# One pool of eight PSUM banks, with dependencies by bank, in a one-core kernel of windowed attention and channel mix

## The chip, the core and the metric

The kernel runs on one core of a Trainium2 chip. The metric is the device time in microseconds of one execution; the lower the better. TensorE (PE) multiplies matrices, ScalarE (ACT) applies functions, VectorE (DVE) does elementwise work, GpSimd (POOL) and SyncE (SP) mainly issue DMAs here. PE writes its results to PSUM, which has eight banks of 512 float32 in each of 128 partitions; ACT and DVE read them from there.

## The reference

Eight batches of eight heads, 576 positions, 64 values a head. Attention looks back over a window of 128 positions and adds a bias that falls with distance; its output is the input of a channel mix with a squared ReLU and a sigmoid gate.

```python
scores = scale * np.matmul(q, k.transpose(0, 1, 3, 2))
scores = np.where((rel >= 0) & (rel < 128), scores + bias, -1e9)
attn = softmax(scores)                       # over the last axis
x = (attn @ v)                               # to [8, 576, 512]
x_prev = x shifted by one position
xk = mu_k * x + (1 - mu_k) * x_prev
xr = mu_r * x + (1 - mu_r) * x_prev
k = np.maximum(xk @ w_k, 0)                  # 512 -> 1024
v = (k * k) @ w_v                            # 1024 -> 512
out = v / (1 + exp(-(xr @ w_r)))
```

## The kernel before

The work of a batch is cut into four pairs of heads. For a pair, PE makes q and k transposed (`qk_quad`, L1070), the scores in two halves of up to 512 columns for each of two heads (`scores`, L698; matmuls at L726, which have 64 rows and run two at a time, and for batch 0 a bias matmul at L713), ACT takes their exponential (L740), DVE multiplies by a table of the bias and the window (L753), PE multiplies by v (`attend`, L759, matmul L781, here called AV), DVE divides by the row sums (L787, L793), PE transposes the result (L820, L837) and ACT copies it (L696). DVE makes the shifted mixes xk and xr (L880, L887). The channel mix (L968) goes over 13 stretches of 256 to 512 positions: eight groups of k matmuls (L983), each with a Relu on ACT (L990) and a square on ACT (L962) or DVE (L964); then for each 128 positions the r matmuls (L1001) with a Tanh on ACT (L1008), the v matmuls (L1017), and one DVE instruction (L1022) that joins the two before the store. At the start PE runs 90 filler matmuls (`warm`, L687) in places of the order.

The order of PE, ACT and DVE is written out by hand: the lists `ORDER` (L22 to L71) name operations by number, and the planner (L88) gives each engine the next one of its list as soon as its operands and buffers are there, so that its clock and its buffers decide which buffer an operation gets (`pick`, L130, `take`, `give`), not the order. The order of DMA issues on POOL and SP is its own choice. An operation asks for buffers by `Hold(class)`. PSUM has two classes: `p2`, the two tiles `duo0` and `duo1` of two banks each, for scores and AV, and `p1`, the four tiles `uno0` to `uno3` of one bank, for the rest (L369 to L383). The framework makes an instruction wait for earlier instructions on other engines that use the same tile. `SS` (L298) says for which batches the two halves of a pair's scores are separate operations in the lists: for none. So both halves stand in one operation, which needs both `duo` tiles.

The lines that the prediction speaks of are those named above and ACT's first table load, which the profile puts at L696.

Of the kernel before, what the change touches and what calls it, by code (L numbers as in the profile page):

```python
# [9 lines left out]
FP32 = mybir.dt.float32  # L10
# [28 lines left out]
""".split()],  # L39
    "ACT": [int(x) for x in """  # L40
# [11 lines left out]
""".split()],  # L52
    "DVE": [int(x) for x in """
# [187 lines left out]
def kernel(  # L241
# [56 lines left out]
    SS = ()  # L298
# [17 lines left out]
    MMASK = False  # L316
# [6 lines left out]

    cst = ctx.enter_context(tc.tile_pool(name="cst", bufs=1))
# [349 lines left out]
    h_mu = Hold("p1")  # L674

    def emit_mu(e):
        nc.tensor.transpose(one(h_mu)[:, 0:2 * NPO], mu_row, id32[0:2 * NPO, 0:2 * NPO])
# [3 lines left out]
    n_muk = n_mur = plan.add(DVE, 0.08, LAT[DVE], [n_mut], (0, 4), lambda e: nc.vector.tensor_copy(  # L681
        out=mu_sb.rearrange("p i o -> p (i o)"), in_=one(h_mu)[:, 0:2 * NPO]), (), [h_mu])

    h_wm = Hold("p1")

    def emit_warm(e):
        nc.tensor.matmul(one(h_wm)[:, 0:128], lhsT=warm, rhs=warm, start=True, stop=True)  # L687
# [7 lines left out]
    def copy_any(e, out, in_):  # L695
        (nc.scalar.copy if e == ACT else nc.vector.tensor_copy)(out=out, in_=in_)  # L696

    def scores(b, g, parts, bias, hq, ha, deps, prio, need, free):  # L698

        todo, dur = [], 0.0  # L700
        for (pieces, m0, tt) in parts:
            a0 = BASE[pieces[0][0]] + pieces[0][1] - 128 * pieces[0][0]
            w = sum(n for _, _, n in pieces)
            todo.append((pieces, m0, tt, a0, w, Hold("p2")))
            dur += sum(max(n / 2400 + .0025, .03) for _, _, n in pieces)
            dur += 0.01 + (2 * mm(w) if bias else 0)
# [24 lines left out]
        s = op(PE, (0.12 if bias else 0.02) + dur, deps, prio + (2,), emit, list(need) + [x[5] for x in todo], free)  # L731
# [27 lines left out]
    def attend(b, g, t0, t1, ha, deps, prio):  # L759
# [3 lines left out]
        hp, hx = Hold("p1" if 2 * nt * W <= 512 else "p2"), Hold("xu")  # L763
# [5 lines left out]
        def a5():  # L769
            if hp.cls == "p1":  # L770
                return one(hp)[:, 0:2 * nt * W].rearrange("p (h t c) -> p h t c", h=2, c=W)
            return two(hp)[:, :, 0:nt * W].rearrange("p h (t c) -> p h t c", c=W)

        def emit(e):
            at, vs, tvb, a = at_buf[ha.idx], vs_buf[hv.idx], tv_buf[hv.idx], a5()
            for t in range(t0, t1):
                for hl in range(2):
                    us = [u for u in (t - 1, t) if u >= 0]
                    for u in us:
                        lo = 1024 * hl + BASE[u] + 128 * (t - u)  # L780
                        nc.tensor.matmul(  # L781
                            a[:, hl, t - t0], lhsT=at[:, lo:lo + 128],
# [3 lines left out]
        def emit_r(e):  # L786
            nc.vector.reciprocal(out=rc_buf[hx.idx][:, :, 0:nt], in_=a5()[:, :, :, D])  # L787

        def emit_x(e):
            rc = rc_buf[hx.idx]  # L790
            out_ = xo().rearrange("p t h d -> p h t d")
            if e == DVE:
                nc.vector.tensor_tensor(  # L793
                    out=out_, in0=a5()[:, :, :, 0:D],
                    in1=rc[:, :, 0:nt, None].to_broadcast([128, 2, nt, D]), op=ALU.mult)
                return
            for t in range(nt):
                for hl in range(2):
                    nc.scalar.activation(out=out_[:, hl, t], in_=a5()[:, hl, t, 0:D],
                                         func=AF.Copy, scale=rc[:, hl, t:t + 1])  # L800
# [527 lines left out]
```

## Time and profile before

| | |
|---|---|
| runs shown | 229.55, 228.80, 229.41 us |
| median | 229.41 us |
| profiled execution: its time | 228.84 us |
| profiled execution: its span | 227.1 us |
| granted TensorE clock | 0.998 |
| PE busy | 221.8 us, 98% of the span |
| DVE busy | 188.8 us, 83% |
| ACT busy | 155.0 us, 68% |
| POOL busy | 92.0 us, 41% |

The span runs from the first to the last instruction; the time of the execution has 1.7 us more around it. The ends of matmuls are modelled, and matmuls are pipelined, so that a matmul's row says more of when it started than of how long PE was taken. The distance from the start of one row to the start of the next, less what the same matmuls take where they follow one another without a gap, is what PE lost there.

### The profile page before, as it was taken

The numbers are of one execution on the slowest core, as the hardware profiler recorded it, in microseconds if no ns is written. First come the engines' busy times: TensorE is split into PE (matmuls) and PEld (weight loads), VectorE is DVE, ScalarE is ACT, GpSimd is POOL, SyncE is SP. The second block draws the span as 40 slices with busy tenths as digits, with TensorE's granted clock in tenths as the row PEclk, the third lists the DMA queues.
The fourth block names the chain that finished last, engine by engine and source line by source line (L and its number), as shares of the span: only waits on it lengthen the run. The fifth ranks groups of instructions, "written<-read, shape, count | busy, mean of one in ns | idle before, by whom it ended". The sixth has DMA issues, their size and how long they took to land.

```text
span 227.1 us, 6442 instructions
## 1 busy us (share of the span) xinstructions
PE 221.8 (98%) x2587; PEld 133.2 (59%) x2587; DVE 188.8 (83%) x423; ACT 155.0 (68%) x279; POOL 92.0 (41%) x118
## 2 busy tenths in 40 slices
PE   8899999999999999999999999999999999999994
PEld 8576766755666755556666554546765455446552
DVE  6786999899879998899978996999899988963433
ACT  0678999999989984975868358768567564047511
POOL 8856726599962964385208750240000000000000
PEclk9999999999999999999999999999999999999999
DMA  6999999999999999999999999999150415430124
GB/s 165 179 185 200 197 196 175 199 180 151 196 156 165 137 130 180 168 182 147 211 180 158 120 185 231 177 136 222 30 135 3 123 46 52 131 136 3 49 92 139
DMA packets 129981, 33.19 MB, mean 146 GB/s; under 512 B 116632, under 2 KB 126112, under 8 KB 129952
## 3 DMA queue, kind: packets, MB, share of 16 engines
q0 software_dynamic: 95728, 16.26, 97.5%
q1 hardware_dynamic: 32480, 15.94, 34.1%
q10 hardware_dynamic: 1744, 0.59, 1.1%
q8 instruction: 20, 0.33, 0.6%
q14 instruction: 9, 0.07, 0.1%
HBM read 33.56 MB, written 9.44 MB: 189 GB/s over the span
## 4 chain that ended last, share of the span: by engine, by line
PE 92%; ACT 3%; DMA 2%; SPq 1%; issue 0%; DVE 0%; DVEq 0%; ACTq 0%
PE uno L983 28%; PE uno L1017 28%; PE uno L1001 13%; PE duo L726 7%; PE duo L781 7%; DMA qx<-in_q_dram 2%; PE uno L837 2%; PE uno L1078 2%; ACT at L740 1%; PE duo L713 1%; ACT qk L696 1%; PE uno L781 1%; SPq L550 1%; PE uno L687 1%; PE uno L820 1%; PE uno L939 0%
## 5 line engine op out<-in xcount | busy, mean ns | idle before, releaser
L983 PE MATMUL uno<-xk,wk_sb 128*128 128x256 bf16 (+2 forms) x416 | 72.0, 314 | 0.1
L740 ACT ACTIVATE at<-duo 128x1024 bf16<-128x1024 f32 (+2 forms) x68 | 65.5, 985 | 8.8 <-PE duo L726 8.5
L1017 PE MATMUL uno<-wv_sb,kk 128*128 128x512 bf16 (+2 forms) x296 | 69.7, 374 | 0.0
L990 ACT ACTIVATE rl<-uno 128x256 bf16<-128x256 f32 (+2 forms) x104 | 46.4, 471 | 26.4 <-PE uno L983 21.0
L983 PEld LDWEIGHTS <-wk_sb 128*128 128x128 bf16 x416 | 38.7, 98 | 24.2 <-issue 0.3
L1017 PEld LDWEIGHTS <-kk 128*128 128x128 bf16 x296 | 27.2, 98 | 27.3
L500 POOL DMA_DIRECT2D vs<-in_v_dram x32 | 28.4, 904 | 31.8 <-PE duo L781 25.9
L753 DVE TENSOR_TENSOR at<-at,mask 128x1024 bf16<-128x1024 bf16 x56 | 36.9, 682 | 1.8 <-ACT at L740 1.8
L964 DVE TENSOR_TENSOR kk<-rl 128x256 bf16<-128x256 bf16 (+2 forms) x94 | 30.2, 339 | 8.8 <-ACT rl L990 8.4
L1008 ACT ACTIVATE rs<-uno 128x512 bf16<-128x512 f32 x36 | 21.1, 604 | 22.2 <-PE uno L1001 22.1
L1001 PE MATMUL uno<-wr_sb,xr 128*128 128x512 bf16 x144 | 36.1, 379 | 0.0
L1022 DVE SCALAR_TENSOR_TENSOR ot<-rs,uno 128x512 f32<-128x512 bf16 (+2 forms) x37 | 24.4, 666 | 10.5 <-PE uno L1017 8.8
L887 DVE SCALAR_TENSOR_TENSOR xk<-dl,mu_sb,xt 128x576 bf16<-128x576 bf16 (+1 forms) x32 | 24.4, 779 | 0.0
L887 DVE SCALAR_TENSOR_TENSOR xr<-dl,mu_sb,xt 128x576 bf16<-128x576 bf16 (+1 forms) x32 | 24.3, 776 | 0.0
L781 PEld LDWEIGHTS <-at 128*128 128x128 bf16 x576 | 21.0, 97 | 4.7 <-ACT at L740 0.4
L793 DVE TENSOR_TENSOR xu<-duo,rc 128x640 bf16<-128x640 f32 x28 | 22.6, 815 | 0.2
L1001 PEld LDWEIGHTS <-xr 128*128 128x128 bf16 x144 | 13.3, 98 | 13.5 <-issue 0.2
L531 POOL DMA_DIRECT2D cb<-in_k_dram x20 | 17.5, 888 | 6.9 <-DMA vs<-in_v_dram 4.7
L781 PE MATMUL duo<-vs,at 128*128 128x65 bf16 x448 | 18.6, 193 | 0.0
L531 POOL DMA_DIRECT2D cb<-in_q_dram x20 | 17.7, 935 | 1.2 <-PE duo L781 1.1
L696 ACT COPY xt<-uno 128x640 bf16<-128x640 bf16 (+3 forms) x28 | 15.0, 583 | 3.3 <-PE uno L837 2.5
L880 DVE TENSOR_TENSOR dl<-xt 128x576 bf16<-128x576 bf16 (+1 forms) x32 | 13.5, 432 | 2.8 <-ACT xt L696 2.7
(83 smaller groups left out, 197.9 us busy)
## 6 DMA issues: line engine op xcount, KB each, us to landing
out_dram<-ot SPq DMA_DIRECT2D x30, 256.0 KB, 4.6
vs<-in_v_dram POOLq DMA_DIRECT2D x32, 128.0 KB, 7.8
cb<-in_q_dram POOLq DMA_DIRECT2D x20, 128.0 KB, 6.3
cb<-in_k_dram POOLq DMA_DIRECT2D x20, 128.0 KB, 12.1
out_dram<-ot SPq DMA_DIRECT2D x10, 128.0 KB, 1.8
wk_sb<-in_moe_w_k_dram POOLq DMA_DIRECT2D x2, 512.0 KB, 9.1
cb<-in_q_dram POOLq DMA_DIRECT2D x4, 256.0 KB, 9.7
cb<-in_k_dram POOLq DMA_DIRECT2D x4, 256.0 KB, 8.6
```

The costliest lines, as they stand in the source:

```text
L500: return dma(POOL, 256, issue_t(1024), lambda e: nc.gpsimd.dma_start(out=vs_buf[h.idx][:, j, :, 0:D], in_=v[b, :, 128 * j:128 * j + 128].r ...
L531: return [dma(POOL, 256, issue_t(1024), lambda e, r=r: nc.gpsimd.dma_start(out=cb_buf[h.idx][:, i, r], in_=src[:, :, r]), [g], kind="q") f ...
L740: lambda e, ah=ah, w=w, hp=hp: nc.scalar.activation(out=ah(), in_=two(hp)[:, :, 0:w], func=AF.Exp, scale=float(scale)), (), [hp])
L753: nc.vector.tensor_tensor(out=a, in0=a, in1=m, op=ALU.mult)
L781: nc.tensor.matmul(a[:, hl, t - t0], lhsT=at[:, lo:lo + 128], rhs=vs[:, u, 2 * g + hl, 0:W] if u < NF else tvb[:, 2 * g + hl, 0:W], start= ...
L887: lambda e: nc.vector.scalar_tensor_tensor(out=buf[hk.idx][:, g, e0 + c0:e0 + c1], in0=dls(), scalar=mu[:, g:g + 1], in1=xc(1), op0=ALU.mu ...
L964: nc.vector.tensor_tensor(out=out, in0=in_, in1=in_, op=ALU.mult)
L983: nc.tensor.matmul(one(hp)[:, 0:n], lhsT=wk_sb[:, po, 128 * fo:128 * fo + 128], rhs=xk_buf[hx.idx][:, po, c0:c1], start=(po == 0), stop=(p ...
L990: a = op(ACT, act_t(n), [s], pr, lambda e, hp=hp, hr=hr: nc.scalar.activation(out=rl_buf[hr.idx][:, 0:n], in_=one(hp)[:, 0:n], func=AF.Rel ...
L1001: nc.tensor.matmul(one(hp), lhsT=xr_buf[hx.idx][:, po, 128 * c:128 * c + 128], rhs=wr_sb[:, po], start=(po == 0), stop=(po == NPO - 1))
L1017: nc.tensor.matmul(one(hv)[:, a:b], lhsT=kk_buf[hk.idx][:, fo, o:o + 128], rhs=wv_sb[:, fo, a:b], start=(fo == 0), stop=(fo == NFO - 1))
L1022: nc.vector.scalar_tensor_tensor(out=ot_buf[ho.idx][:, a:b], in0=rs_buf[hs.idx][:, a:b], scalar=1.0, in1=one(hv)[:, a:b], op0=ALU.add, op1 ...
```

## The change

PSUM becomes four tiles of two banks, `duo0` to `duo3`, and one class `p` of eight banks. An operation asks for one bank or for a pair (0, 2, 4 or 6 and the next one). `pick` gives a single bank from a pair of which the other bank is taken, where there is one. What each operation needs is as before: two banks for a score half and for a batch's AV, one for the rest.

Two operations can now use the two banks of one tile. `use()` tells the framework that an instruction that uses one bank does not depend on instructions of other engines that use the other one. The helpers `matmul`, `transpose` and `copy_of` apply it; so PE's lines in the new kernel are those of the helpers, L395 and L398. Scores and AV, which use whole tiles, are left as they were.

```diff
-    SS = ()
+    SS = range(1, B)
...
-    duo = [pst.tile([128, 2, 512], FP32, name=f"duo{i}") for i in range(2)]
-    uno = [pst.tile([128, 512], FP32, name=f"uno{i}") for i in range(4)]
-    N1 = 4
-    PT = "p1"
+    duo = [pst.tile([128, 2, 512], FP32, name=f"duo{i}") for i in range(4)]
 
     def one(h):
-        return uno[h.idx if h.cls == "p1" else N1 + h.idx]
+        return duo[h.idx // 2][:, h.idx % 2]
 
     def two(h):
-        return duo[h.idx]
-
-    plan = Plan(dict(qx=2, p2=2, p1=N1, pt=4 - N1, qk=NQ, at=NA, xu=NX, vs=NV, cb=NC, ts=2, tt=2, xt=2, dl=2, dl0=4,
+        return duo[h.idx // 2]
+
+    shared = {}
+
+    def use(h, x, other=None):
+        if h.n == 1:
+            here = x.ins.engine
+            both = shared.setdefault((other.cls, other.idx), []) if other else []
+            for e in (ENG.PE, ENG.Activation, ENG.DVE):
+                if e != here:
+                    tc.declare_no_dep(x.ins, group=f"{e}{h.idx ^ 1}", keep=both,
+                                      reason="the tile's other bank")
+            tc.add_to_no_dep_group(f"{here}{h.idx}", x.ins)
+            if other:
+                both.append(x.ins)
+        return x
+
+    def matmul(h, *a, **k):
+        return use(h, nc.tensor.matmul(*a, **k))
...
+    plan = Plan(dict(qx=2, p=8, qk=NQ, at=NA, xu=NX, vs=NV, cb=NC, ts=2, tt=2, xt=2, dl=2, dl0=4,
                      xk=2, rl=3, kk=3, rs=4, ot=NO),
-                {}, WAIT)
+                {"p": (0, 2, 4, 6)}, WAIT)
...
-            todo.append((pieces, m0, tt, a0, w, Hold("p2")))
+            todo.append((pieces, m0, tt, a0, w, Hold("p", 2)))
...
-        hp, hx = Hold("p1" if 2 * nt * W <= 512 else "p2"), Hold("xu")
+        hp, hx = Hold("p", 1 if 2 * nt * W <= 512 else 2), Hold("xu")
...
-            hp, hr = Hold("p1"), Hold("rl")
+            hp, hr = Hold("p"), Hold("rl")
```

With `SS = range(1, B)` the halves of a pair's scores are separate operations from batch 1 on, each with a pair of banks of its own. Code that no setting used (`mask_pe`, `qk_full`) goes. The three lists are new as a whole; their first lines on PE, for the look of them:

```diff
-105 101 76 85 128 75 52 119 121 46 117 98 47 65 40 51 81 68 97 88 122 84 41 112 48 120 72 93 82 94 77 45 63 100
+39 106 68 112 113 93 63 47 96 57 110 81 105 76 123 103 124 125 54 86 79 114 128 67 100 66 92 78 115 120 72 43
```

What the two kernels issue is the same: 2587 matmuls, and the same instructions in all. Four squares (two of 128x256, two of 128x384) and one copy of 128x512 that DVE did are now ACT's. Along PE's list the shape of the array changes 98 times between one matmul and the next, before 107 times. PE has 438 instructions with a wait for another engine, before 442.

Three places of the lists. The first is ACT's start, where batch 0 is worked off; `at` takes the exponential of scores, `qk` is q and k transposed, `xt` the transposed output. Before:

```order
L696 CAST qk2_73<-uno1_126 128x2x256 [waits PE_49]
L740 ACTIVATE at0_77<-duo0_123 128x2x384
L740 ACTIVATE at1_78<-duo1_124 128x2x384 [waits PE_49]
L740 ACTIVATE at2_79<-duo0_123 128x2x384 [waits PE_49]
L740 ACTIVATE at0_77<-duo1_124 128x2x384 [waits PE_49,Activation_49]
```

And now, from the same point:

```order
L716 COPY qk0_71<-duo3_126 128x2x256 [waits PE_49]
L763 ACTIVATE at0_77<-duo0_123 128x2x384 [waits DVE_49,PE_49]
L763 ACTIVATE at1_78<-duo1_124 128x2x384 [waits DVE_49,PE_49]
L716 CAST qk3_74<-duo3_126 128x2x256 [waits DVE_49,PE_49]
L763 ACTIVATE at2_79<-duo0_123 128x2x384 [waits PE_49]
L763 ACTIVATE at0_77<-duo1_124 128x2x384 [waits PE_49,Activation_49]
```

A copy that DVE made stands first, and the first two exponentials stand ahead of the cast, which reads q and k that came in last.

The second is on PE in the channel mix of the last stretch of the first two batches, at the ninth group of r matmuls of the program. Before, the group stands behind an AV and a group of k matmuls, and writes a tile of its own class:

```order
L781 MATMUL duo0_123<-tv0_65,at0_77 128x65
L983 LDWEIGHTS wk_sb_116
L983 MATMUL uno2_127<-xk0_93,wk_sb_116 128x256 [waits DVE_49]
...
L1001 LDWEIGHTS xr0_95
L1001 MATMUL uno3_128<-wr_sb_118,xr0_95 128x512 [waits Activation_49]
```

Now it stands behind the two halves of a pair's scores and four v matmuls, and writes a bank of the tile that the first half was in:

```order
L749 MATMUL duo0_123<-tt1_70 128x64
L749 LDWEIGHTS qk2_73
L749 MATMUL duo1_124<-qk2_73 128x256 [waits Activation_49]
...
L395 MATMUL duo3_126<-wv_sb_117,kk0_100 128x512
...
L395 LDWEIGHTS xr0_95
L395 MATMUL duo0_123<-wr_sb_118,xr0_95 128x512 [waits Activation_49]
```

What the group waits for was the Tanh or Relu that had read `uno3`; it is now the exponential of the scores just ahead of it.

The third is the end of PE's list, where the last v matmuls stand in two parts, of 384 columns and of 128. Before:

```order
L1001 MATMUL uno2_127<-wr_sb_118,xr1_96 128x512
L1017 LDWEIGHTS kk2_102
L1017 MATMUL uno3_128<-wv_sb_117,kk2_102 128x384
...
L1017 MATMUL uno0_125<-wv_sb_117,kk2_102 128x128 [waits DVE_49]
```

And now:

```order
L395 MATMUL duo3_126<-wr_sb_118,xr1_96 128x512
L395 LDWEIGHTS kk2_102
L395 MATMUL duo3_126<-wv_sb_117,kk2_102 128x384
...
L395 MATMUL duo3_126<-wv_sb_117,kk2_102 128x128 [waits Activation_49]
```

The part of 128 columns takes the bank of the last r, and so waits for the last Tanh.

More of the change, by code (lines that the diff above doesn't have):

```diff
@@ L670 @@
         op0=ALU.mult), [n_ident], (0, 2 + h)) for h in range(H)]
-    h_mu = Hold("p1")
+    h_mu = Hold("p")
     def emit_mu(e):
-        nc.tensor.transpose(one(h_mu)[:, 0:2 * NPO], mu_row, id32[0:2 * NPO, 0:2 * NPO])
+        transpose(h_mu, one(h_mu)[:, 0:2 * NPO], mu_row, id32[0:2 * NPO, 0:2 * NPO])
     n_idr = dve_op(0.21, lambda e: nc.vector.tensor_copy(out=id32, in_=ident), [n_ident], (0, 3))
     n_mut = plan.add(PE, 0.12, LAT[PE], n_row + [n_idr], (-1e6, 0), emit_mu, [h_mu])
-    n_muk = n_mur = plan.add(DVE, 0.08, LAT[DVE], [n_mut], (0, 4), lambda e: nc.vector.tensor_copy(
-        out=mu_sb.rearrange("p i o -> p (i o)"), in_=one(h_mu)[:, 0:2 * NPO]), (), [h_mu])
-    h_wm = Hold("p1")
+    n_muk = n_mur = plan.add(DVE, 0.08, LAT[DVE], [n_mut], (0, 4), lambda e: use(h_mu, nc.vector.tensor_copy(
+        out=mu_sb.rearrange("p i o -> p (i o)"), in_=one(h_mu)[:, 0:2 * NPO])), (), [h_mu])
+    h_wm = Hold("p")
     def emit_warm(e):
-        nc.tensor.matmul(one(h_wm)[:, 0:128], lhsT=warm, rhs=warm, start=True, stop=True)
+        matmul(h_wm, one(h_wm)[:, 0:128], lhsT=warm, rhs=warm, start=True, stop=True)
     g_wm = plan.add(VIR, 0.0001, 0.0001, [], (0,), None, [h_wm])
@@ L695, in copy_any, with copy_of @@
     def copy_any(e, out, in_):
-        (nc.scalar.copy if e == ACT else nc.vector.tensor_copy)(out=out, in_=in_)
+        return (nc.scalar.copy if e == ACT else nc.vector.tensor_copy)(out=out, in_=in_)
+    def copy_of(h, e, out, in_):
+        return use(h, copy_any(e, out, in_))
     def scores(b, g, parts, bias, hq, ha, deps, prio, need, free):
@@ L730, in scores @@
             dur *= 1.6
-        s = op(PE, (0.12 if bias else 0.02) + dur, deps, prio + (2,), emit, list(need) + [x[5] for x in todo], free)
+        s = op(PE, (0.12 if bias else 0.01 * len(parts)) + dur, deps, prio + (2,), emit, list(need) + [x[5] for x in todo], free)
         s.rows = (128 if bias else 64, 64)
@@ L812, in out_t @@
         n = c1 - c0
-        hp = Hold(PT if b else "p1")
+        hp = Hold("p")
         def tp():
@@ L938, in emit @@
                 for hl in range(2):
-                    nc.tensor.matmul(
-                        one(hp)[64 * hl:64 * hl + 64, 64 * n:64 * n + 64],
+                    matmul(
+                        hp, one(hp)[64 * hl:64 * hl + 64, 64 * n:64 * n + 64],
                         lhsT=ts_buf[hs.idx][:, n],
@@ L978, in channel_mix @@
         for fo in range(NFO):
-            hp, hr = Hold("p1"), Hold("rl")
+            hp, hr = Hold("p"), Hold("rl")
             def emit(e, fo=fo, hp=hp):
                 for po in range(NPO):
-                    nc.tensor.matmul(
-                        one(hp)[:, 0:n], lhsT=wk_sb[:, po, 128 * fo:128 * fo + 128],
+                    matmul(
+                        hp, one(hp)[:, 0:n], lhsT=wk_sb[:, po, 128 * fo:128 * fo + 128],
                         rhs=xk_buf[hx.idx][:, po, c0:c1], start=(po == 0),
@@ L1007, in channel_mix @@
             t = op(ACT, act_t(512), [s], pr,
[L1008 to L1010 removed]
+                   lambda e, hp=hp, hs=hs: use(hp, nc.scalar.activation(
+                out=rs_buf[hs.idx], in_=one(hp), func=AF.Tanh, scale=0.5), hs), [hs], [hp])
+            hv, ho = Hold("p"), Hold("ot")
             o = 128 * c - c0
@@ L1166, in make_mask @@
                              func=AF.Exp, scale=-(2.0 ** (-(h + 1))))
-    def mask_pe(j):
-        hp = Hold("p2")
-        def emit(e):
-            for h in range(4):
-                nc.tensor.matmul(two(hp)[:, h // 2, 256 * (h % 2):256 * (h % 2) + 256],
-                                 lhsT=sid[:, 4 * j + h], rhs=dist[:, 0:256],
-                                 start=True, stop=True, skip_group_check=True)
-        m = op(PE, 4 * mm(256), [n_dist] + n_sid[4 * j:4 * j + 4] + gate, (2, 2 * j), emit, [hp])
-        return op(ACT, act_t(1024), [m], (2, 2 * j + 1), lambda e: nc.scalar.activation(
-            out=mask[:, 4 * j:4 * j + 4, 0:256],
-            in_=two(hp).rearrange("p b (h c) -> p (b h) c", h=2), func=AF.Exp,
-            scale=float(scale)), (), [hp])
-    if MMASK:
-        ms = [mask_pe(j) for j in range(2)]
-    else:
-        ms = [op(ACT, act_t(256, True), [n_dist] + gate, (2, h), lambda e, h=h: make_mask(h))
-              for h in range(H)]
+    ms = [op(ACT, act_t(256, True), [n_dist] + gate, (2, h), lambda e, h=h: make_mask(h))
+          for h in range(H)]
     n_mcopy = []
@@ L1223, in qk_some @@
         return res
-    def qk_full(b, g, prio):
-        hp, hq = Hold(PT), Hold("qk")
-        hc = ch[b]
-        def emit_t(e):
-            for n in range(2 * NF):
-                nc.tensor.transpose(
-                    one(hp).bitcast(BF16)[:, 128 * n:128 * n + 128],
-                    cb_buf[hc.idx][:, n // NF, n % NF, 2 * g:2 * g + 2].rearrange(
-                        "p h d -> p (h d)"), ident)
-        t = op(PE, 0.0565 * 8, cl[b], prio + (3,), emit_t, [hp, hq], [hc])
-        y = op(ACT, act_t(1024), [t], prio + (3,), lambda e: copy_any(
-            e, qk_buf[hq.idx].rearrange("p t (c r) -> p t c r", r=NF),
-            one(hp).bitcast(BF16).rearrange("p (t r c) -> p t c r", t=2, r=NF)), (), [hp])
-        return hq, [y]
     for b in range(1, B):
```

114 lines of the change are left out of this document (55 added, 59 removed), and 84 rows, old and new, of the table ORDER.

## The prediction

> **What bounds the kernel.** I read the page first: the busy shares, the slices, the chain.
>
> ```profile
> PE 221.8 (98%) x2587; PEld 133.2 (59%) x2587; DVE 188.8 (83%) x423; ACT 155.0 (68%) x279; POOL 92.0 (41%) x118
> PE   8899999999999999999999999999999999999994
> PE 92%; ACT 3%; DMA 2%; SPq 1%; issue 0%; DVE 0%; DVEq 0%; ACTq 0%
> ```
>
> PE is the bound from the second slice to the last, 92% of the chain is its own, and the matmuls are the same in number and shape after. So the change can only alter three things: what PE waits, what its changes of array shape cost, and what lies behind its last matmul. I then asked who waited for whom (PE shows two waits, at its first filler and for the first loads), and went to the rows of single stretches, because the modelled end of a matmul covers short gaps. There I go by starts. PE's prices where nothing is missing come from rows like these:
>
> ```profile
> 93.22 2.97 PE L983 MATMUL uno<-xk,wk_sb 128*128 128x512 bf16 x13
> 70.17 1.04 PE L1017 MATMUL uno<-wv_sb,kk 128*128 128x512 bf16 x4
> 71.04 1.03 PE L1001 MATMUL uno<-wr_sb,xr 128*128 128x512 bf16 x4
> 26.95 0.60 PE L983 MATMUL uno<-xk,wk_sb 128*128 128x256 bf16 x4
> 27.39 0.39 PE L912 MATMUL uno<-ident,ts 128*128 128x128 bf16 x4
> 27.83 0.33 PE L820 MATMUL uno<-ident,xu 128*128 128x128 bf16 x3
> ```
>
> Four matmuls of 512 columns take 71.04 - 70.17 = 0.87 us, 0.216 each; four of 256 take 0.44, so 0.109 each; a 128 column one is then some 0.055. The four of 128 at 27.39 should take 0.22, but the next row starts 0.44 behind: **0.22 us lost**, without a word in the waits.
>
> **Where PE loses time before.** Nearly all such places lie ahead of 33 us. The rows of the largest, beside those above:
>
> ```profile
> 7.99 1.06 PE L1123 MATMUL uno<-id,qx 128*128 128x128 f32 x7 [0.48 <-DMA qx<-in_q_dram]
> 9.63 0.29 PE L687 MATMUL uno<-warm 128*128 128x128 bf16 x2
> 10.00 0.49 PE L713 MATMUL duo<-dist,sid 128*128 128x384 bf16 x2
> 12.28 0.44 PE L687 MATMUL uno<-warm 128*128 128x128 bf16 x5
> 12.84 0.24 PEld L781 LDWEIGHTS <-at 128*128 128x128 bf16 x6 [0.29 <-ACT at L740]
> 14.17 0.40 PE L1078 MATMUL uno<-ident,qx 64*64 64x64 bf16 x16
> 14.51 0.40 PE L687 MATMUL uno<-warm 128*128 128x128 bf16 x4
> 15.06 0.57 PE L1078 MATMUL uno<-ident,qx 64*64 64x64 bf16 x16
> 15.56 0.50 PE L713 MATMUL duo<-dist,sid 128*128 128x384 bf16 x2
> ```
>
> Two fillers, 0.11 us, fill 9.63 to 10.00: 0.26 lost. Five, 0.28, fill 12.28 to 12.84: 0.28 lost. The 16 small transposes took 0.34 at 14.17 and 0.50 at 15.06: 0.16 lost. With the 0.22 above, **0.92 us** that are not the load's (which is the 0.48 of the first row, and stays: the load is the same). A few smaller ones bring it to an estimate of 1.4 us by 33 us.
>
> Why is the third bias matmul late at 10.00? It needs `duo0`, so the exponential of the first scores must have read it:
>
> ```profile
> 6.28 1.28 ACT L696 ACT_TABLE_LOAD   x1 [6.28 <-DVE qk L696]
> 6.73 0.34 PE L726 MATMUL duo<-qk 64*128 64x256 bf16 x4
> 8.65 0.59 ACT L696 CAST qk<-uno 128x512 bf16<-128x512 f32 x1 [1.08 <-PE uno L1123]
> 9.13 2.48 ACT L740 ACTIVATE at<-duo 128x768 bf16<-128x768 f32 x3
> ```
>
> The scores were done by about 7.1, the table by 7.56; yet the exponential starts at 9.13, behind a cast that waits for the load.
>
> **Start of batch 0: -0.8 us.** The new list has the exponential ahead of that cast, behind one copy that DVE did (0.6 us by the cast's row). It can start at 7.56 + 0.6 = 8.2, 0.9 earlier. The 0.26 goes whole, and the 0.28 at 12.84, an AV that waited for an exponential, as far as 0.9 us of lead carries through a stretch in which ACT stays full. The fillers now stand mostly ahead of the first scores; they were in gaps, so that costs nothing. What is late next is the staged load and the exponentials behind it: by the same arithmetic on the new order, three gaps of some 0.2 to 0.3 us stay, 0.75 in all. 1.4 - 0.75 = 0.65, and 0.15 more for a smaller lead that the staged q and k ask of PE. The bounds: nothing (all gaps return elsewhere) and 1.6.
>
> **Changes of shape: -0.8 us.** Between 64 and 128 rows a change has a price:
>
> ```profile
> 96.12 0.56 PE L726 MATMUL duo<-qx 64*128 64x256 bf16 x8
> 99.66 0.56 PE L726 MATMUL duo<-qx 64*128 64x256 bf16 x8
> 100.08 0.19 PE L726 MATMUL duo<-tt 64*128 64x64 bf16 x2
> 100.20 1.04 PE L1001 MATMUL uno<-wr_sb,xr 128*128 128x512 bf16 x4
> ```
>
> From 93.22, 13 matmuls by 0.216 give 2.81; the next row starts 2.90 behind: 0.09. From 100.08 two small ones, one behind the other 0.03 at most, take 0.12 to the next shape: again 0.09. The order has 98 changes for 107, so 9 x 0.09 = 0.8 off, all on PE and under no cover. The bounds are nothing (the changes that go stood where PE waited anyway) and 9 x 0.16 = 1.5, if what a change costs is the whole time by which a matmul's row (1.04 for four of 512 columns, so 0.39 for the last of them behind 3 x 0.216) outlasts its stream of 0.22.
>
> The Trainium skill, TensorEngine Tiling (Array Packing), section Tiling Modes, Key Properties, says that a change of the tiling mode, not of the tile, drains the TensorE. Placing the halves alone invites more changes, so that rule speaks against the change as an idea; the trace agrees that a change costs, at 0.09 us a time, which is less than emptying the array by the modelled ends would be; by a full drain the term would be its bound of 1.5. The order has fewer changes, not more, so here the rule works for the change.
>
> **New short waits: +0.6 us.** With one pool an operation gets the bank that came free last, often straight from an exponential. The r group of the change's second place stands behind both halves of a pair's scores and four v matmuls. Cover of PE from the end of the first half: the second half, 0.22 (both together took 0.44 at 99.66), the change of shape 0.09 and four v, 0.87, in all 1.18. What it waits for:
>
> ```profile
> L740 ACT ACTIVATE at<-duo 128x1024 bf16<-128x1024 f32 x56 | 56.7, 1036 | 8.2 <-PE duo L726 8.2
> 221.69 1.03 PE L1001 MATMUL uno<-wr_sb,xr 128*128 128x512 bf16 x4
> 222.76 0.60 ACT L1008 ACTIVATE rs<-uno 128x512 bf16<-128x512 f32 x1 [3.72 <-PE uno L1001]
> ```
>
> The last r, from 221.69, streams until 222.55, and its Tanh starts at 222.76: 0.21 from PE to ACT. With 1.04 of exponential and an estimated 0.05 back that is 1.30, so 0.12 short. Queued behind are the other three r and all of PE. The same sum over the new order, with each reader's duration from its rows, finds eight more places behind 33 us that are short by about as much, so 1.1. Before had a few too:
>
> ```profile
> 46.24 0.39 PE L912 MATMUL uno<-ident,ts 128*128 128x128 bf16 x4
> 46.59 1.02 PE L1001 MATMUL uno<-wr_sb,xr 128*128 128x512 bf16 x4
> 58.97 0.60 PE L983 MATMUL uno<-xk,wk_sb 128*128 128x256 bf16 x4
> 59.52 0.62 PE L781 MATMUL duo<-vs,at 128*128 128x65 bf16 x15
> ```
>
> 0.35 for 0.22 and 0.55 for 0.44: 0.24 lost in two, and an estimated 0.5 in all. Net +0.6; the bounds are 0 and twice the nine less those, 1.7.
>
> **Five instructions from DVE to ACT: 0.** ACT's squares, and three stretches (behind the length: PE, weight loads, DVE, ACT, POOL):
>
> ```profile
> L962 ACT ACTIVATE kk<-rl 128x256 bf16<-128x256 bf16 x9 | 3.6, 428 | 0.0
> L962 ACT ACTIVATE kk<-rl 128x384 bf16<-128x384 bf16 x1 | 0.5, 516 | 0.0
> 20.00:60.00 40.00, 39.85 (x713) 26.05 (x713) 37.42 (x82) 38.84 (x78) 28.78 (x36) 1.00 1.82 188
> 36.00:60.00 24.00, 24.00 (x429) 15.41 (x428) 22.75 (x44) 23.07 (x44) 20.86 (x26) 1.00 1.98 185
> 60.00:190.00 130.00, 130.00 (x1427) 75.50 (x1424) 116.62 (x238) 93.34 (x155) 48.31 (x58) 1.00 1.47 145
> ```
>
> Two squares by 0.43, two by 0.52 and a copy by 0.60 are 2.5 us more of ACT by its rows, and that much less of DVE. From 20 to 60 us ACT is busy 38.84 of 40, so 1.16 is free there; DVE has 2.58. From 60 to 190 ACT has 36 us free. The squares lie between, from the first to the third channel mix. I price them at nothing: eight banks let PE run on while ACT is late, up to the time it has for free behind 60 us. If that cover is gone, see the slower case.
>
> **End: +0.05.** The last matmuls and what joins their results:
>
> ```profile
> 222.56 1.26 PE L1017 MATMUL uno<-wv_sb,kk 128*128 128x384 bf16 x12
> 223.47 0.75 DVE L1022 SCALAR_TENSOR_TENSOR ot<-rs,uno 128x384 f32<-128x384 bf16 x2 [0.88 <-PE uno L1017]
> ```
>
> The last v part waits for the last Tanh, done at 222.76 + 0.60 = 223.36. Before, that part started behind four of 384 columns (0.16 each, three quarters of 0.216): 222.56 + 0.65 = 223.2. So 0.2 late. But the joining of the first part (DVE L1022) starts only behind the Tanh as well, at 223.47, and the second joins behind it, so most of the 0.2 is covered; between 0 and 0.2.
>
> **Sum.** -0.8 - 0.8 + 0.6 + 0.05 = -0.95 on the profiled execution's 228.84 us (its span of 227.1 and 1.7 around it): 227.9. That execution lies at the low end of the runs, 0.6 below their median of 229.41; I put the new median half of the way up as one profile is no better than another run, 0.25: **228.1 us**, 0.6% below.
>
> **Rivals.**
> - *All of the start's gaps go* and the short waits do not come, because banks picked from eight have usually been free for long: -1.6 - 0.8 + 0.1 = -2.3, so 226.5 in the profile and about 226.8. For it: most gaps are 0.1 to 0.3 us, so a little lead closes them. Against: ACT is full from 7 to 60 us, and a lead there does not grow. 0.12.
> - *Nothing to be seen.* The waits only change places: 438 for 442 is no sign that waits went, since one-bank tiles already kept most operations apart. The start gives 0.3, the waits take 1.1 (nothing of before's goes), the shapes give 0.8: 228.8 in the profile, 229.1 as a median. 0.27.
> - *Slower: ACT becomes the bound between 20 and 60 us.* Its 2.5 us more do not fit into 1.16 us free, and the exponential of each half must now come before its two banks serve k, r or v. From the point at which ACT is later than the time that banks already written give PE (some 1.2 us of cover in the r group above), PE waits for every Relu. Then 2.5 - 1.16 = 1.3 us come on top, and the short waits double, +1.1: 227.9 + 2.4 = 230.3, a median of about 230.5. Against it: DVE is relieved by as much, and its multiplies stand in the same chain. 0.15.
>
> **How the numbers follow.** The forecast, 227.3 to 228.7, has 0.46. A measurement of this kernel tells 0.3%, 0.7 us, from no change, so below 228.7 is faster: 0.46 + 0.12 = 0.58; within 0.27; slower 0.15. The range has to hold 8 in 10, and the bounds of the terms (-1.6 - 1.5 + 0 below, 0 + 0 + 1.7 + 0.2 above, not all at once) reach to both rivals: 226.5 to 230.3.
>
> **What would show it.** In the changed profile the first exponential starts near 8.2, and the bias matmul at 10.00 has no gap ahead of it. Stretches of 64 rows stand with fewer joints. At the ninth r group the start distance behind the four v is about 0.12 over 0.87. ACT has less than 1 us free from 20 to 60, and PE still runs 24 of 24 there. If PE shows waits for Relu or for scores' exponentials of half a microsecond in that stretch, the slower case is right; if PE's first 33 us are not shorter, the term of the start was wrong.

## The result, and the profile after

| | before | changed |
|---|---|---|
| median of 20 runs | 229.41 us (228.80 to 229.70) | 229.59 us (229.19 to 230.65) |
| profiled execution, time and span | 228.84, 227.1 | 230.64, 228.5 |
| time around the span | 1.7 to 1.85 in every execution | 2.06 to 2.18 in every execution |

The ratio of changed to before is 1.0017 (1.0007 to 1.0027): no gain, but a loss of some 0.2%. In a later comparison on one chip it was 1.0031 (1.0016 to 1.0046), 229.83 to 229.06. The prediction was 228.1. The profiled execution of the changed kernel is one of its longest, which is of use here, since what makes it long can be seen in it. Its page:

```profile
PE 221.7 (97%) x2587; PEld 132.0 (58%) x2587; DVE 187.2 (82%) x418; ACT 155.3 (68%) x284; POOL 92.1 (40%) x118
PE   8899989979999999999999999999999999999994
PE 94%; DMA 3%; issue 1%; SPq 1%; DVE 0%; DVEq 0%
```

PE is the bound as before, but two of its slices have holes, and "issue" is now 1% of the chain. The list of PE's waits, in us, times, longest, has a row that the kernel before did not have:

```profile
PE duo L398 <- issue: 1.8, 2, 1.1
PE duo L395 <- DVE warm L489: 1.0, 1, 1.0
PE duo L398 <- DMA qx<-in_q_dram: 0.7, 1, 0.7
PE duo L398 <- DVE qk L716: 0.3, 1, 0.3
```

"issue" means that the profile shows nothing that PE waited for. The timeline of PE has the two places:

```profile
29.03 0.38 PE L398 MATMUL duo<-ident,cb 64*64 64x64 bf16 x22
30.05 0.28 PE L398 MATMUL duo<-ident,cb 64*64 64x64 bf16 x10 [0.64 <-issue]
...
49.90 0.25 PE L398 MATMUL duo<-ident,cb 64*64 64x64 bf16 x7
51.27 0.40 PE L398 MATMUL duo<-ident,cb 64*64 64x64 bf16 x25 [1.11 <-issue]
51.60 1.04 PE L395 MATMUL duo<-wv_sb,kk 128*128 128x512 bf16 x4
```

Both times PE stops inside one operation, 22 and 7 transposes into 32 that read one loaded buffer and write two banks that it already writes. No load, bank or reader can be missing there. Counted from start to start, less what these transposes take elsewhere, the stops are 0.82 and 1.30 us, 2.1 in all.

The start, on ACT and PE:

```profile
2.90 1.28 ACT L716 ACT_TABLE_LOAD   x1 [2.90 <-issue]
6.49 0.58 ACT L716 COPY qk<-duo 128x512 bf16<-128x512 bf16 x1 [2.31 <-PE duo L398]
7.76 0.81 ACT L763 ACTIVATE at<-duo 128x768 bf16<-128x768 f32 x1 [0.69 <-PE duo L749]
10.01 0.81 ACT L763 ACTIVATE at<-duo 128x768 bf16<-128x768 f32 x1 [1.44 <-PE duo L749]
7.38 0.34 PE L749 MATMUL duo<-qk 64*128 64x256 bf16 x4
8.69 0.68 PE L398 MATMUL duo<-id,qx 128*128 128x128 f32 x3 [0.71 <-DMA qx<-in_q_dram]
10.23 0.66 PE L398 MATMUL duo<-id,qx 128*128 128x128 f32 x4 [0.26 <-DVE qk L716]
```

The first exponential starts at 7.76, 1.4 earlier than before, but the second only at 10.01: PE's second scores now stand behind a load for which PE waits until 8.69, and what PE lost to exponentials it loses here to the load and to a copy on DVE.

The place of the ninth r group, and the end:

```profile
82.52 1.04 PE L395 MATMUL duo<-wv_sb,kk 128*128 128x512 bf16 x4
83.47 1.02 PE L395 MATMUL duo<-wr_sb,xr 128*128 128x512 bf16 x4
...
224.04 1.46 PE L395 MATMUL duo<-wv_sb,kk 128*128 128x384 bf16 x12
224.24 0.60 ACT L1031 ACTIVATE rs<-duo 128x512 bf16<-128x512 f32 x1 [4.33 <-PE duo L395]
224.94 0.87 DVE L1045 SCALAR_TENSOR_TENSOR ot<-rs,duo 128x384 f32<-128x384 bf16 x2 [0.91 <-PE duo L395]
```

From the v group to the r group there are 0.95 us where four v take 0.87: 0.08 lost to the exponential, 0.12 forecast. At the end the last part waits 0.20 for the Tanh (1.46 for 1.26 us), and what follows PE is shorter by as much.

### The profile page after: what moved, and what is told of

It reads as the page before. It is cut to its first block, busy times and chain, and to the rows that moved or that the text cites. A ratio compares the mean times of both kernels' runs of the same rounds, so it can differ in the third digit from the quotient of the medians.

```text
span 228.5 us, 6437 instructions
## 1 busy us (share of the span) xinstructions
PE 221.7 (97%) x2587; PEld 132.0 (58%) x2587; DVE 187.2 (82%) x418; ACT 155.3 (68%) x284; POOL 92.1 (40%) x118
## 4 chain that ended last, share of the span: by engine, by line
PE 94%; DMA 3%; issue 1%; SPq 1%; DVE 0%; DVEq 0%
PE duo L395 79%; PE duo L749 8%; PE duo L398 6%; DMA qx<-in_q_dram 3%; PE duo L736 1%; SPq L570 1%; DVE qk L716 0%; DVE ot L1045 0%; DVEq L716 0%
## 5 line engine op out<-in xcount | busy, mean ns | idle before, releaser
L395 PE MATMUL duo<-xk,wk_sb 128*128 128x256 bf16 (+2 forms) x416 | 70.6, 313 | 0.0
L395 PE MATMUL duo<-wv_sb,kk 128*128 128x512 bf16 (+2 forms) x296 | 69.8, 374 | 0.0
L1013 ACT ACTIVATE rl<-duo 128x256 bf16<-128x256 f32 (+2 forms) x104 | 45.3, 477 | 34.1 <-PE duo L395 30.4
L395 PEld LDWEIGHTS <-wk_sb 128*128 128x128 bf16 x416 | 38.9, 98 | 23.4 <-issue 1.2
L395 PEld LDWEIGHTS <-kk 128*128 128x128 bf16 x296 | 27.0, 98 | 28.9 <-issue 1.3
L1031 ACT ACTIVATE rs<-duo 128x512 bf16<-128x512 f32 x36 | 21.3, 599 | 22.6 <-PE duo L395 17.2
L395 PE MATMUL duo<-wr_sb,xr 128*128 128x512 bf16 x144 | 36.2, 379 | 0.0
L1045 DVE SCALAR_TENSOR_TENSOR ot<-rs,duo 128x512 f32<-128x512 bf16 (+2 forms) x37 | 24.4, 663 | 8.8 <-PE duo L395 4.2
L816 DVE TENSOR_TENSOR xu<-duo,rc 128x640 bf16<-128x640 f32 (+2 forms) x36 | 26.6, 743 | 0.5
L395 PEld LDWEIGHTS <-at 128*128 128x128 bf16 x576 | 21.7, 97 | 5.0 <-issue 0.3
L395 PE MATMUL duo<-vs,at 128*128 128x65 bf16 x512 | 22.1, 193 | 0.0
L395 PEld LDWEIGHTS <-xr 128*128 128x128 bf16 x144 | 13.2, 97 | 13.8 <-issue 0.8
L716 ACT COPY xt<-duo 128x512 bf16<-128x512 bf16 (+3 forms) x28 | 15.6, 588 | 0.9 <-PE duo L398 0.8
L716 ACT COPY qk<-duo 128x512 bf16<-128x512 bf16 (+1 forms) x24 | 12.8, 563 | 4.1 <-PE duo L398 4.1
```

The costliest lines, as they stand in the source:

```text
L395: return use(h, nc.tensor.matmul(*a, **k))
L716: return (nc.scalar.copy if e == ACT else nc.vector.tensor_copy)(out=out, in_=in_)
L816: use(hp, nc.vector.tensor_tensor(out=out_, in0=a5()[:, :, :, 0:D], in1=rc[:, :, 0:nt, None].to_broadcast([128, 2, nt, D]), op=ALU.mult), hx)
L1013: a = op(ACT, act_t(n), [s], pr, lambda e, hp=hp, hr=hr: use(hp, nc.scalar.activation(out=rl_buf[hr.idx][:, 0:n], in_=one(hp)[:, 0:n], fun ...
L1031: lambda e, hp=hp, hs=hs: use(hp, nc.scalar.activation(out=rs_buf[hs.idx], in_=one(hp), func=AF.Tanh, scale=0.5), hs), [hs], [hp])
L1045: use(hv, nc.vector.scalar_tensor_tensor(out=ot_buf[ho.idx][:, a:b], in0=rs_buf[hs.idx][:, a:b], scalar=1.0, in1=one(hv)[:, a:b], op0=ALU. ...
```

## The experiments

**Theory and rival.** The page of the changed kernel counts 20 packets of "q8 instruction" with 0.33 MB, 16.4 KB each, as that of before does:

```profile
q8 instruction: 20, 0.33, 0.6%
```

PE has 5193 rows in the trace (weight loads, matmuls and 19 rows of its sequencer), some 20 times 256. (The Trainium skill, Perfetto Trace Analysis, section Per-instruction lifecycle, The 4-stage abstract model, has an instruction at 64 bytes; 256 of them are 16.4 KB, and the packets agree.) In PE's order the two stops stand ahead of rows 961 and 1729, counted from 0, which is 3 x 256 apart. The theory is that **PE's own instructions come by DMA in blocks of 256**, the next one being asked for about when a block is entered, and that PE stops at a border if it has run through a block faster than that takes. The rival is that the stops belong to the work that stands there.

The profile's DMA view of the 1.1 us about such a packet, in the changed kernel:

```profile
q0 software_dynamic: 1051, 0.13, 190.0%
q8 instruction: 1, 0.02, 5.3%
```

One packet of instructions, among 1051 of the loads that POOL issues (190% is the mean over the core's 16 DMA engines of the time that packets took, and packets overlap). By the packets' own records and PE's starts:

| execution | block entered | packet starts | packet ends | PE goes on in the next | PE's work in the block |
|---|---|---|---|---|---|
| before | 44.77 | 47.05 | 48.02 | 49.61, no stop | 4.84 |
| changed | 24.40 | 27.55 | 28.44 | 30.05 | 4.81 |
| changed | 45.40 | 48.90 | 49.83 | 51.27 | 4.56 |

The stop ends 1.4 to 1.6 us behind the packet. Before, PE needed 4.84 us for its fastest block, and the instructions were there, by a hair: PE used them 1.59 behind the packet. The new order puts more small transposes and AV matmuls side by side, and two of its blocks are run through in 4.8 and 4.6.

The traces of all 16 runs kept here bear this out (in six of them rows of matmuls are missing, and there the rows are counted by the weight loads). With borders at row 193 and every 256 rows on, each block has one packet, which starts between 1.9 us ahead of PE's entry into it and 4.9 us behind. At 304 borders PE never goes on sooner than 1.26 us behind the packet's end, and the 16 stops, all ahead of row 961 or 1729, end 1.26 to 1.60 behind it.

**The borders moved.** The first fillers, split in two, move all later work along the stream and cost no columns:

```diff
-        matmul(h_wm, one(h_wm)[:, 0:128], lhsT=warm, rhs=warm, start=True, stop=True)
+        filled.append(0)
+        for c in (0, 64) if len(filled) <= 48 else (0,):
+            w = 64 if len(filled) <= 48 else 128
+            matmul(h_wm, one(h_wm)[:, c:c + w], lhsT=warm, rhs=warm[:, c:c + w], start=True, stop=True)
```

> The changed kernel with the first 48 fillers issued as two matmuls of 64 columns instead of one of 128, so that the same work of PE is 96 instructions further along its stream; columns and filler time are the same. Theory (PE's instructions come by DMA in blocks of 256, about 5.3 us after PE enters the block before; PE stops where it runs through a block faster): the block borders fall elsewhere, two blocks take 4.1 us (near 25 us) and 2.4 us (near 47 us) by the profile's starts, so PE stops there for about 1.2 and 2.9 us, without a releaser in the profile; in all some 4 us against 2.1 in the profile of the changed kernel, a time of 231.5 to 232.5. Rival (the two stops of the profile belong to the work that stands there, a load or a bank): they stay at the same transposes, 229.6.

Measured: 233.6 us, 1.020 of before (1.017 to 1.023). PE's waits and the two places:

```profile
PE duo L398 <- issue: 2.6, 1, 2.6
PE duo L395 <- issue: 1.7, 5, 1.0
```

```profile
26.71 0.27 PE L395 MATMUL duo<-xk,wk_sb 128*128 128x256 bf16 x1
27.94 0.50 PE L395 MATMUL duo<-xk,wk_sb 128*128 128x256 bf16 x3 [0.96 <-issue]
```

```profile
46.74 0.41 PE L398 MATMUL duo<-ident,cb 64*64 64x64 bf16 x27
49.77 0.27 PE L398 MATMUL duo<-ident,cb 64*64 64x64 bf16 x5 [2.63 <-issue]
```

The stops left the transposes of the changed kernel, which now run through, and stand 96 instructions earlier in the work: one inside a group of four k matmuls, one in other transposes. They are 1.12 and 2.81 us; 1.2 and 2.9 were computed from the changed kernel's starts. That is the theory's result, and the rival falls. (The median is 1.1 us above the range given, which the theory does not explain. The trace shows a likely cause: behind the stop of 2.81, from 49.6 to 53.0 us, the granted clock is 0.50, for 1.00 before and after. Half of these 3.4 us, 1.7, is an estimate of the most that it costs. One of the four runs has a trace; the mean clocks of all four, 0.985 to 0.992 for 0.998 to 1.0 in the changed kernel, fit it.)

The same done to the kernel before, with 52 fillers split, and with 32 joined to 16 of 256 columns:

> The kernel before with the first 52 fillers split in the same way. Theory: borders fall so that no block between 10 and 60 us is run through in less than 5.3 us, where two now take 4.9; what the kernel before loses in its slower executions goes, 0.2 to 0.5 us less, about 229.0, and a narrower spread. Rival: 229.4, no change.

> The kernel before with the first 32 fillers issued as 16 of 256 columns, so that the work stands 32 instructions earlier in the stream. Theory: one block, entered near 40 us, is run through in 4.4 us, so PE stops there for some 0.5 to 1.0 us without a releaser: 229.8 to 230.3. Rival: 229.4, no change.

Measured: split 229.81 us, ratio 1.0011 (0.9999 to 1.0024); joined 229.45, ratio 1.0029 (1.0001 to 1.0057), with executions up to 232.3 (the ratios leave out one of 235.3 and one of 776). Neither came as expected. The profile of the split one shows why the forecast was too simple:

```profile
47.73 0.31 PE L1083 MATMUL uno<-ident,cb 64*64 64x64 bf16 x14
48.98 0.34 PE L1083 MATMUL uno<-ident,cb 64*64 64x64 bf16 x18 [0.93 <-issue]
```

Here the kernel before has a stop too, 1.11 us, again ahead of row 1729. Its block takes PE 5.44 us, which I had put beyond danger; but the packet started 4.22 us behind the block's entry, and the stop ended 6.56 behind it. In the joined one the fastest block took 4.35 us without a stop, since its packet started after 1.34. So it is not one limit of 5.3 us: from entry to use were 4.7 to 6.6 us where PE had to wait, and most of the difference is when the packet starts. That it stands behind the loads in a queue is likely, but no run shows it.

**One more profile of the changed kernel**, and one with two small instructions more on GpSimd (for the time around the span):

> The changed kernel once more, for a second profile. Theory (instruction blocks that come late by the state of the DMA queues): PE stops at the same two places of its stream, near 30 and 51 us, by other lengths than 0.8 and 1.3 us, and the execution's time follows their sum: 228.6 us plus the stops. Rival (the stops are of the one execution profiled): none, at 229.6.

> The changed kernel with two memsets of one column more at the end of GpSimd's stream, which brings its length from 189 to the 191 instructions of the kernel before. In all executions so far of the changed kernel and its variants with 189 instructions on GpSimd the time has 2.1 us around the span, in all others (191, 144 or 142 there) 1.8. If GpSimd's length is the cause: 1.8 around the span, 0.35 less, 229.25. Rival (something else of the change): 2.1, 229.6.

```diff
                 n.emit(n.eng)
+        for _ in range(2):
+            nc.gpsimd.memset(spare, 0.0)
```

Measured: 229.83 us, and 229.74, ratios 1.0031 (1.0016 to 1.0046) and 1.0013 (0.9998 to 1.0029). Both profiled executions stop at the same two places, by other lengths. The second profile of the changed kernel, then the one with the memsets:

```profile
30.03 0.28 PE L398 MATMUL duo<-ident,cb 64*64 64x64 bf16 x10 [0.52 <-issue]
...
49.89 0.64 PE L398 MATMUL duo<-ident,cb 64*64 64x64 bf16 x32
```

```profile
49.88 0.25 PE L399 MATMUL duo<-ident,cb 64*64 64x64 bf16 x7
50.98 0.40 PE L399 MATMUL duo<-ident,cb 64*64 64x64 bf16 x25 [0.85 <-issue]
```

| execution | time | around the span | PE from first to last start | stops | PE without them | time without them |
|---|---|---|---|---|---|---|
| before | 228.84 | 1.77 | 222.61 | 0 | 222.61 | 228.84 |
| changed | 230.64 | 2.11 | 224.28 | 2.12 | 222.16 | 228.52 |
| changed, again | 229.52 | 2.11 | 223.14 | 0.87 | 222.27 | 228.65 |
| with two memsets | 230.03 | 1.78 | 224.00 | 1.71 | 222.29 | 228.32 |

The times without the stops agree within 0.15 us for the changed kernel, as the theory had it. And GpSimd's stream is what makes the 0.35: with 191 instructions there for 189 all 12 executions have 1.73 to 1.83 around the span. The median is not the 229.25 expected, and only 0.09 below that of the changed kernel in the same comparison: the span was longer, by stops that differ from execution to execution as far as the profiles tell. (The traces have one row less of GpSimd each, 190 and 188.) Why two more at its end shorten what lies around the span, no run shows.

**Fewer loads.** The loads of v for batches 2 to 7 left out, in both kernels (they multiply by the v of an earlier batch):

```diff
-        return dma(POOL, 256, issue_t(1024), lambda e: nc.gpsimd.dma_start(
+        return dma(POOL, 256, issue_t(1024), lambda e: None if b > 1 else nc.gpsimd.dma_start(
```

> The changed kernel without the loads of v for batches 2 to 7 (it multiplies by the v of an earlier batch that still lies there): 24 of the 32 loads of 128 KB gone, PE's work the same. Theory: with less of other transfers ahead of them the instruction blocks come sooner, and the two stops without a releaser go: 1.0 to 1.5 us less than the changed kernel, about 228.4. Rival (the stops are not of PE's instructions): 229.6 unless a load of q or k is what PE waits for, in which case a releaser shows.

> The kernel before without the loads of v for batches 2 to 7 (it multiplies by the v of an earlier batch), as was done to the changed kernel, which then took 229.14. Theory: the kernel before has little to lose in instruction stops, so it gains at most 0.4: 229.0 to 229.3, and its profile has no stop without a releaser of over 0.3 us. Rival (fewer loads help PE by themselves): it gains as the changed kernel did or more, 228.7 or less.

Measured: changed 229.14 us, ratio 0.9994 (0.9980 to 1.0008); before 229.35, ratio 0.9999 (0.9984 to 1.0015). The changed kernel's stops were 0.58 and 0.47, less than in its first profile but not gone, and in sum more than in its second; and 0.35 of what it gained is the time around the span, which with 142 instructions on GpSimd is 1.8. It missed the 228.4 expected, and proves little. Then with no load of v but batch 0's (all batches multiply by that one):

> The kernel before with no load of v but batch 0's: all batches multiply by the v of batch 0. Theory: it has no instruction stops to lose, so 228.8 to 229.3.

> The changed kernel with no load of v but batch 0's. GpSimd has 134 instructions, so 1.8 us around the span. Theory: the instruction blocks come sooner, the stops shrink from 0.9 to 2.1 us to 0 to 0.5, and what the change gains otherwise is seen: 228.3 to 228.7, 0.4 to 0.8 below the kernel before with the same loads left out. Rival (the change gains nothing even without stops): 229.0 to 229.3, as the kernel before.

Measured: before 229.48 us, ratio 1.0016 (0.9997 to 1.0034); changed 229.18, 1.0012 (0.9994 to 1.0031). The stops were not made away with: 0.67 and 0.70 in the changed kernel, and one of 0.44 in the kernel before, at row 1729. The packets started as late as ever (2.8 to 3.3 us behind the entry), and from 44 to 51 us the DMA engines were as full (a share of 2.13 and 2.16, for 2.18 in the changed kernel): the loads that are left fill the freed time. The time of the changed one lies where the rival had put it, but with stops of 1.4 us in it that decides nothing. What the change is worth without stops is thus not measured; the table above gives it by subtraction.

**The work of the two blocks spread.** In PE's list four v matmuls go ahead of the transposes near 50 us; the first attempt also put r matmuls ahead of those near 29, the second put r ahead of the next scores, and the third adds the memsets:

```diff
-... 322 99 263 122 369 327 336 209 278 ... 463 319 510 315 501 483 317 320 ...
+... 322 99 263 122 278 369 327 336 209 ... 463 319 315 510 501 483 317 320 ...
```

```diff
-... 463 319 510 315 501 483 317 320 ...
+... 463 319 315 510 317 501 483 320 ...
```

> The changed kernel with two entries of PE's list moved: four v matmuls of 512 columns go ahead of the 32 small transposes near 50 us, and four r matmuls of 512 columns ahead of the 32 near 29 us, so that each of the two blocks of 256 instructions in which PE stopped holds 0.87 us more of work. Theory (PE's instructions come too late in those two blocks): of the 2.1 us of stops in the changed kernel's profile 1.3 to 1.7 go, the time falls by 0.7 to 1.2 to about 228.7, below both kernels. Rival (the stops go with those transposes or their loads): no gain, or a loss from copies that come later, 229.6 to 230.

> The changed kernel with the four v matmuls ahead of the 32 small transposes near 50 us, as in the spread tried first, and four r matmuls behind those transposes and ahead of the scores, so that the copies of the transposes have as much cover as before; the place near 29 us is left alone. Theory: the second stop shrinks from 1.3 to at most 0.4 and nothing new waits, 0.5 to 0.9 less than the changed kernel, 228.7 to 229.1. Rival (the copies and scores come too late again): 229.6 or more, with waits for ACT's copies near 53 us.

> Both of the last two: the sum of their gains, 228.4 to 228.8, below the kernel before by 0.3 to 0.4%. Rival: the sum of whatever they show apart.

Measured: 231.83 us (1.0105, 1.0085 to 1.0125), 234.45 (1.0234, 1.0207 to 1.0260), 234.54 (1.0226, 1.0207 to 1.0245). The stops of the blocks that were spread are gone, as the theory says: none at either place in the first, only that near 30 in the others. But the move opens other waits: PE comes sooner to things that are not there yet, or the moved matmuls no longer cover what they covered. PE's waits in the first, and in the second:

```profile
PE duo L733 <- ACT qk L700: 1.5, 1, 1.5
PE duo L379 <- DVE warm L473: 1.0, 1, 1.0
PE duo L379 <- DMA wr_sb<-in_moe_w_r_dram: 0.7, 1, 0.7
```

```profile
PE duo L733 <- DVE ot L1029: 3.5, 1, 3.5
```

The copies of the later transposes, the load of the weights of r, and a bank that DVE frees late cost 1.7, 0.9 and 3.8 us from start to start (the first two in the first attempt, the third in the second). Behind the 3.8 the granted clock is 0.50 for 3.4 us, as it was behind the stop of 2.81. So moving two entries did not mend the list, and no version here beats the kernel before.

**The parts of the change.** The declared independence taken away, all else left:

```diff
-        if h.n == 1:
+        if False:
```

> The changed kernel without the declared independence: an instruction that uses one bank waits for earlier instructions of other engines on the tile's other bank too; the lists and the banks are the same. If that independence carries the pool: PE waits for readers of the other bank all through, several us more, 233 to 240. Rival, as in the prediction's case of nothing to be seen (the order keeps the two banks of a tile apart anyway): within 0.5 us of 229.6.

Measured: 260.09 us, 1.134 (1.131 to 1.136), a loss three times the most that I gave. Two users of one tile's two banks thus need the declaration. PE then waits all through for readers of the other bank; the first rows of its waits:

```profile
PE duo L395 <- ACT rs L1031: 5.6, 10, 1.1
PE duo L395 <- ACT rl L1013: 4.8, 9, 0.7
PE duo L398 <- ACT rs L1031: 2.3, 3, 0.9
```

And the start's edit alone, in the kernel before:

```diff
-10 11 12 13 14 156 134 147 169 ...
+10 11 12 13 14 134 147 156 169 ...
```

> The kernel before with one entry of ACT's list moved: the cast that waits for the second load of q and k stands behind the first two exponentials, as in the changed kernel. By the prediction's term of the start: the first exponential starts near 7.6, the gap of 0.24 us ahead of the third bias matmul goes and part of the 0.28 near 12.8, so 0.3 to 0.5 us less, about 229.0. Rival (the cast is then late, and what it feeds): the gaps before 20 us stay at 1.2 us in sum, 229.4.

Measured: 229.25 us, ratio 0.9996 (0.9981 to 1.0010). In its profile the gap of 0.24 ahead of the third bias matmul is gone and that near 12 shrank to 0.23; PE from first to last start is 222.45 for 222.61, a gain of 0.16 where 0.3 to 0.5 was expected, too small for the comparison of times to tell.

## Why the prediction was wrong, by its steps

**The step that failed** is the one that bounded the case: that "the change can only alter three things: what PE waits, what its changes of array shape cost, and what lies behind its last matmul". There is a fourth, the speed at which PE's instructions come. The prediction gave it no term, and the new order runs into it twice. The runs show 0.9, 1.7 and 2.1 us of it in three executions of the new order; the medians of 229.59 and 229.83 against about 228.6 without stops put the usual sum near 1.1, which is an inference from the table. A reader of the trace of before could have found the fastest block: 4.84 us there, with its packet's end 1.6 us ahead of use.

**The time around the span** was taken as 1.7 for both. It is 0.35 more in the changed kernel, and this term too was put at nothing without a reason.

The terms themselves, from the starts of all of PE's rows in the profiles of before and of the changed kernel's second one, without the stops:

- Start, to 36 us: PE lost 2.45 before and 2.00 after, -0.45; -0.8 was forecast, inside its bounds. The exponential went ahead (7.76, forecast 8.2), and the gaps at 10.00 and 12.84 went. But the sum for it was not what happened: it let the table load end at 7.56, and the row above has it over at 2.90 + 1.28 = 4.18, so that the exponential waited for PE's scores alone (0.69). These came later than before, from 7.38 us in the first profile and 7.93 in the second, for 6.73. The fillers ahead of them, which were to cost nothing, are 65 for 61, and they start 0.107 us apart until the granted clock goes from 0.50 to 1.00, 0.055 behind that. It went up at 4.09 us in the profile of before, at 4.96 and 6.12 in these two, and between 3.8 and 6.7 in all profiles here, so part of this is chance. What was late next was named, the staged load, but its price was taken too low: in the second profile PE waits 0.94 from start to start, up to 10.32, for the copy on DVE that follows the load. Its row in that profile's waits:

```profile
PE duo L398 <- DVE qk L716: 0.9, 1, 0.9
```

- Short waits: +0.16 from 36 to 60 us and +0.16 from 60 to 190, so +0.3 for +0.6. The mechanism was right at the place worked out, 0.08 for 0.12.
- Changes of shape: the price of one held. In the changed kernel too four v matmuls ahead of a matmul of 64 rows take 81.74 - 80.78 = 0.96 for 0.87, so 0.09 (the rows below). Nine changes fewer are then worth 0.8, as forecast. What is left when the losses are taken from PE's sum is -0.5, in which shapes and losses too small to count stand together.

```profile
80.78 1.04 PE L395 MATMUL duo<-wv_sb,kk 128*128 128x512 bf16 x4
81.74 0.56 PE L749 MATMUL duo<-qk 64*128 64x256 bf16 x8
```

- End: 0.28 more lost on PE from 190 us, 0.20 of it for the Tanh, and 0.20 less behind it: +0.1 for +0.05.
- Five instructions on ACT: nothing, as priced. From 20 to 60 us ACT (the fourth pair below) was busy 37.59 of 40 in the first profile, of which PE stood still for 2.1, and 38.84 in the second, as full as before. That less than 1 us would be free there did not come:

```profile
20.00:60.00 40.00, 38.20 (x694) 25.56 (x695) 35.53 (x76) 37.59 (x81) 28.50 (x36) 1.00 1.84 184
```

The sum of these, some -0.55, is a gain in the direction of the forecast and not quite two thirds of its -0.95, and the table agrees: 228.65, less the 0.34 around the span, is 0.53 below 228.84. The two things left out take it and more. Of the rivals, "nothing to be seen" came nearest to the time (229.1), but not for its reason: it had new waits of 1.1 take the gain, and 0.3 were found. The slower case named 20 to 60 us, where the loss is, but laid it on ACT.

That 0.25 us was added for a profile at the low end of the runs went the right way for the kernel before, whose median is 0.57 above that profile; what makes this spread, no run shows. For the changed one the stops are a cause that can be named, and the comparison without stops is with that one low profile of before.

## What to carry to other kernels

Where one engine is busy nearly all the time with small instructions, look at how fast it runs through its own stream: a row "issue" inside an operation, always the same number of instructions apart, was a wait for instructions here, and no list of tiles and semaphores shows it. Then the order of the work sets a rate, not only dependencies: many small matmuls side by side while the DMA queues are full cost more here than the same matmuls among large ones. And matmuls moved to cure such a stop leave open what they covered where they stood.

## What the runs showed of the hardware

- PE's stream came in blocks of 256 instructions; all 16 stops lay ahead of row 961 or 1729, whatever work stood there.
- From PE's entry into a block to the use of the block behind it were 4.7 to 6.6 us where PE had to wait, 0.9 of it the packet itself and 1.3 to 1.6 behind its end, while the DMA engines were busy with POOL's loads.
- With 189 instructions on GpSimd the time around the span was 2.06 to 2.18 us, with 191, 144, 142, 136 or 134 it was 1.72 to 1.85, in 49 executions of the one and 187 of the others.
- Behind pauses of PE of 2.8 and 3.8 us the granted clock was 0.50 for 3.4 us; behind those of 1.8 us and less it stayed at 1.00. At the start, fillers of 128 columns were 0.107 us apart until it went to 1.00, and 0.055 behind that.
- A change from 128 to 64 rows cost PE 0.09 us, before and after the change of the kernel.
